# LayerNorm output turned by DMA in blocks 2 to 4 of an S4 + GeGLU layer, with six single PSUM banks and a new order

## The chip, the cores and the metric

The kernel runs on one core of a Trainium2 chip. The core has a matmul engine (TensorE, PE in the profile, with its weight loads as PEld), VectorE (DVE), ScalarE (ACT), GpSimd (POOL) and SyncE (SP), which issues most of the transfers; 16 DMA engines move the data. Each engine works through its own list of instructions in order. The metric is the time of one execution on the device, in microseconds (us), as the median of the runs.

## The reference

One layer of a state-space model with adaptive LayerNorm: length 2048, width 448, state 256, hidden width 1792.

```python
mod = (silu(c) @ w_mod).reshape(c.shape[0], 6, 1, -1)
sa, ca, ga, sb, cb, gb = (mod[:, 0], ..., mod[:, 5])
h = layernorm(x) * (1 + ca) + sa
# A: K[d, l] = Re sum_n C * exp(dt * A * l) * dt * B, then a causal convolution of h with K by FFT, + h * Dskip
x = x + ga * A(h)
h = layernorm(x) * (1 + cb) + sb
# B: gelu(h @ w_gate) * (h @ w_up) @ w_down
x = x + gb * B(h)
```

All inputs and the output are float32.

## The kernel before

**The front** makes the convolution filters K from tables (sine, cosine, exponent on ACT, products on DVE, sums on PE), transforms h and K, multiplies and transforms back. `k_fft` is the part of it that the change touches: for three frequencies at a time it multiplies a filter spectrum in PSUM (pk) with the input spectrum (ut), in `prod`, with one DVE multiply for each of two copies of the input.

**The back** is the gated network, in four blocks of 512 positions; the text calls them blocks 1 to 4, the code has `blk` 0 to 3. For each block, `conv_out` finishes the convolution on PE (co.mm, `yi` times `ai`), adds it to x and takes the LayerNorm (co.add, co.rt, co.rc, co.n) in four parts j of 128 positions. The normalised rows xn (positions on the partitions) must then be turned so that the width lies on the partitions, and split into two fp16 halves, high and low, for exact products: the tile `ht`, 128 x (8 groups of columns) x 4 parts x 128 positions. Block 1 turns float32 rows on PE and splits after (co.t, co.h, co.l). Blocks 2 to 4 split first, into `hl` (high half by ACT or DVE, co.h2; low half by DVE, co.l2), and turn the eight 128x128 fp16 squares on PE with the identity `idenh` into a PSUM tile pt (co.t2, `tr16`); one ACT or DVE copy brings pt to ht (co.c2).

`gate_up` then makes 14 tiles of 128 hidden units: gate and up products on PE in two PSUM banks (pq), GELU on ACT, product on DVE into fq, fp16 split into hh and hlo (`hg`). `down_first` (block 1) and `down` (the others) multiply with w_down; `down` saves matmuls by sums of quarters, in seven products dn0 to dn6 that share three banks. Gate and up weights are split once, kept in DRAM (w_d) and loaded again for each block (wr<-w_d).

**The order** is not the code's. Every step is given to a planner (`Plan`) with an estimated cost for the engines that could run it, what it depends on, and the tiles that it uses; a table `LEAD` shifts the priority of each kind of step, `LEAN` its choice between ACT and DVE. The planner walks through an imagined execution and writes each engine's list of instructions. PSUM has eight banks: in the back, 2 of pt, 2 pairs of pq, 2 of pd (conv-out and down).

The line numbers of the profile before are those of this code:

Of the kernel before, what the change touches and what calls it, by code (L numbers as in the profile page):

```python
# [39 lines left out]
    "anc": -11.71, "ang": -3.44, "bn": 2.2, "c.ai": 5.1, "c.ak": 11.34, "c.au": 12.5, "c.c": 9.28, "c.ea": -19.79,  # L40
    "c.id": -13.24, "c.ih": -0.48, "c.ld": 6.17, "c.rd": -9.5, "co.add": 158.93, "co.adde": -601.4,
    "co.addl": 221.1, "co.addx": 274.52, "co.c2": -159.69, "co.h": 1162.42, "co.h2": -38.47, "co.l": 75.87,
    "co.l2": -285.37, "co.mm": 1062.5, "co.mme": -3.27, "co.mml": 286.81, "co.mmx": 500.21, "co.n": -262.48,
    "co.nx": -202.79, "co.rc": 141.8, "co.rcx": 932.59, "co.rt": 19.25, "co.rtx": -646.04, "co.t": 495.31,
    "co.t2": -516.32, "cos": 5.17, "cos2": 15.48, "d.hi": 901.84, "d.ld": 145.61, "d.lo": 186.95, "d0": -1.9,
# [3 lines left out]
    "e.f": -83.54, "e.hi": 186.89, "e.ld": 60.75, "e.lo": -179.4, "ev.end": -14.36, "ev.fp": -2.28, "ev.geg": 7.98,  # L49
    "ev.ub": -1.24, "f.fc": -5.91, "f.fwd": 10.64, "f.inv": 3.75, "f.pr": -22.92, "f.st": -1.52, "f.ut": 3.93,  # L50
    "f.z": 6.62, "gs": 6.11, "gu": 492.6, "gu.g": -553.63, "gu.h0": 585.93, "gu.ha": -745.69, "gu.hs": -215.61,
    "gu.l0": -34.07, "gu.la": -409.31, "gu.ls": 228.5, "gu.m": 128.51, "gu.s": -35.53, "gu2": -791.75, "ka": 22.04,
    "kd": -6.07, "kev": 9.93, "kgen": 14.34, "kout": 18.8, "lt0": -6.27, "lt1": 1.35, "m.ev": -4.31, "m.ld": 12.22,
# [4 lines left out]
    "p.q31": 2.88, "p.q32": -17.5, "p.q33": -6.64, "pad": 14.21, "rcp": 3.06, "rstd": 1.67, "silu": 10.66,  # L58
    "sin": 8.04, "sin2": 21.53, "t.fc": 12.26, "t.fwd": -1.68, "t.inv": 4.48, "t.p0": -3.04, "t.p1": -11.75,
    "t.st": -18.59, "t.u": 6.08, "t.z": 9.25, "tx": 2.71, "tyc": 5.88, "tys": 1.61, "ua": -6.43, "ua.ev": -7.17,  # L60
    "ua.st": -3.05, "ub": 21.06, "ub.ev": 16.13, "ub.fc": -8.54, "ub.st": 6.94, "ub.u": 2.75, "w.hi": -6.17,
    "w.ld": 2.03, "w.lo": -8.97, "warm": 9.58, "wr.ld": -4.52, "wr.st": 12.94, "x.exp": 2.24, "x.ld": 10.88,
    "x.mm": -1.83, "x1.ld": 7.86, "y.exp": 6.27, "y.mm": -1.56, "yi.d00": -4.27, "yi.d01": 7.83, "yi.d10": -18.27,
    "yi.d11": -8.15, "yi.e": -7.12, "yi.l0": -7.58, "yi.l1": 7.22, "yi.ld": -12.53,
}
LEAN = {
    "co.c2": -0.272, "co.h": -0.408, "co.h2": -0.264, "f.z": -0.511, "kev": -0.043, "kout": -0.269, "mag": -0.072,
    "p.q0": -0.54, "p.q2": -0.299, "p.q30": -0.133, "p.q32": 0.295, "t.z": -0.367, "ua.ev": 0.406, "ub.ev": -0.643,
# [24 lines left out]
class Plan:  # L93


    TABLE, HOP, STICK, RATE = 1.3, 0.3, 5.57, 280.0
# [90 lines left out]
def constants():  # L187
# [45 lines left out]
    for i, e in enumerate(EORD):  # L233
# [35 lines left out]
        "k_ih": np.eye(128, dtype=np.float16),  # L269
# [4 lines left out]
def s4_geglu(ctx: ExitStack, tc: tile.TileContext, a: dict, out: bass.AP):  # L274
# [51 lines left out]
                 "ak0": 1, "ak1": 1, "tp": 4, "w": WST, "yi": 1, "x1": 2, "pd": 2, "pt": 2, "pq": 2,  # L326
                 "ht": 1, "xn": 3, "hl": 2, "ge": 2, "fq": 2, "hg": 1, "wr": WR})
# [545 lines left out]
    def ev_end():  # L873
# [6 lines left out]
        K2["ih"] = POOLS["yp"].tile([128, 128], HF, name="idenh", bufs=1)  # L880
# [7 lines left out]
    def k_fft(grp, bi):  # L888
# [28 lines left out]
        def prod():  # L917
            for t in range(2):
                V.tensor_mul(pp.tile[:, t, :ne], ut.tile[:, t, :ne], pk.tile[:, :ne])  # L919
# [19 lines left out]
        t4 = add("f.pr", {"DVE": 1.22 * f}, v, prod, [t3, t2], [], [pk, ut, pp])  # L939
# [214 lines left out]
    def conv_out(blk, t_x, t_y):  # L1154
# [55 lines left out]
        for j in range(4):  # L1210
            xn, pt, hl = Buf("xn"), Buf("pt"), Buf("hl")
# [6 lines left out]
            def tr(pt=pt, xn=xn):  # L1218
                pt.tile = POOLS["ps"].tile([128, 4, 128], FT, name="pt")
                for k in range(3):  # L1220
                    T.matmul(pt.tile[:, k], xn.tile[:, 128 * k:128 * k + 128], K2["id"], start=True, stop=True)
                for h in range(2):
                    T.matmul(pt.tile[64 * h:64 * h + 64, 3], xn.tile[:, 384:], K2["id"], start=True, stop=True)
# [17 lines left out]
            def tr16(pt=pt, hl=hl):  # L1241
                pt.tile = POOLS["ps"].tile([128, 8, 128], HF, name="pt")
                for k in range(8):
                    T.transpose(pt.tile[:, k], hl.tile[:, 128 * k:128 * k + 128], K2["ih"])
# [20 lines left out]
    def gate_up(blk, f, half=None):  # L1265
# [8 lines left out]
        pb, gb = Buf("pq"), Buf("ge")  # L1274
# [9 lines left out]
        def mm():  # L1284
            ht = hb.tile.rearrange("p k j t -> p k (j t)")
            pb.tile = [POOLS["ps"].tile([128, 512], FT, name=f"pq{k}") for k in range(2)]

            def pair():
                for k in range(2):
                    r = slice(64 * k, 64 * k + 64)  # L1290
                    T.matmul(pb.tile[k][:, ts], wr.tile[r, 3, k, c0:c0 + 128], ht[r, 7, ts],  # L1291
# [3 lines left out]
            for k in range(2):  # L1295
                for i, (m, lo, t) in enumerate(full):
                    T.matmul(pb.tile[k][:, ts], wr.tile[:, 4 * lo + t, k, c0:c0 + 128], ht[:, m, ts],  # L1297
# [4 lines left out]
        def gelu():  # L1302
            gb.tile = POOLS["wk"].tile([128, 512], FT, name="ge")
            A.activation(gb.tile[:, ts], pb.tile[0][:, ts], AF.Gelu_apprx_tanh, scale=1.0 / WS)  # L1304

        def mul():
# [3 lines left out]
            src = [x[:, ts].rearrange("p (h t) -> p h t", t=256) for x in (gb.tile, pb.tile[1])]  # L1310
# [14 lines left out]
        def lo(c):  # L1325
            V.tensor_sub(hg.tile[1][:, cb, c], fq.tile[:, c], hg.tile[0][:, cb, c])  # L1326
        t1 = add("gu" + n, {"PE": 4.4 * w + 0.29}, v, mm, cps + WT[blk, cb] + [GU.get((blk, "g"))], [pb], [hb, wr])
        t2 = add("gu.g", {"ACT": 0.18 + 0.42 * w}, v + 0.9, gelu, [t1], [gb], [pb], table=GELU)
        t3 = add("gu.m", {"DVE": 0.15 + 0.54 * w}, v + 0.9, mul, [t2] + GU.get((blk, cb), []), [fq] if new else [],
                 [gb, pb] + ([] if new else [fq]))  # L1330
# [22 lines left out]
    def down_first(j):  # L1353
# [4 lines left out]
        def mm():  # L1358
            (hh, hl), (dh, dl) = hg.tile, W["d"]
            pb.tile = POOLS["pd"].tile([128, D], FT, name="pd")  # L1360
            ts = slice(128 * (j % 2), 128 * (j % 2) + 128)
            for p in range(7):
# [6 lines left out]
        def res():  # L1369
# [3 lines left out]
        t1 = add("dn", {"PE": 7.95}, v, mm, [GU[0, "l", p] for p in range(7)] + [WT["d", i] for i in range(7)] +  # L1373
                 [GU.get((0, "d"))], [pb], [hg])
# [4 lines left out]
    def down(blk):  # L1379

        hg, xb, pb, ab = HG[blk], X1[blk], Buf("pq"), Buf("pd")
# [3 lines left out]
        def bank(k):  # L1385
            return (ab.tile if k == 2 else pb.tile[k])[:, :D].rearrange("p (m d) -> p m d", m=2)

        def mm(i, q, k, new, ps):
            (hh, hl), (dh, dl) = hg.tile, W["d"]
            if i == 0 and ps[0] == 0:  # L1390
                pb.tile = [POOLS["ps"].tile([128, 512], FT, name=f"pq{x}") for x in range(2)]
                ab.tile = POOLS["pd"].tile([128, D], FT, name="pd")
# [22 lines left out]
        def prod(i, q, k, new, deps, v_, al=(), use=(), ps=range(7)):  # L1415
            return add("dn%d" % i, {"PE": 0.565 * len(ps)}, v + v_, lambda: mm(i, q, k, new, list(ps)), deps + wd, al, list(use) + [hg])

        def kept(n, k, deps, v_):
            b = Buf("xn")
            return b, add("dn.k" + n, {"ACT": 0.55}, v + v_ + 0.02, lambda: keep_(k, b), deps, [b], [ab if k == 2 else pb])  # L1420

        def out_(n, src, h, c, deps, v_):
# [3 lines left out]
                    [xb, ab if src[-1] == 2 else pb] + ([] if one else [ob]))  # L1426
# [7 lines left out]
        p1 = prod(0, (0, 0), 0, True, la[:6] + [g], 0.0, [pb, ab], (), range(6))  # L1434
        p1 = prod(0, (0, 0), 0, False, la[6:] + [p1], 0.1, (), [pb], (6,))
# [129 lines left out]
```

## Time and profile before

| | us |
|---|---|
| median of three runs | 831.16 |
| their range | 828.82 to 837.64 |
| the profiled execution | 839.22 |
| its span, first to last instruction | 837.4 |
| PE busy | 752.7 (90%) |
| DVE busy | 606.6 (72%) |
| ACT busy | 463.4 (55%) |
| block 2's part of the back, 541.8 to 640.8 us | PE busy 99.0 of 99.0 |

A row of the profile names the line, the engine, the operation, and what it writes and reads by the program's names (pq<-ht,wr is a matmul of ht with wr into pq). SPq rows are SP's issues of transfers. "Idle before" is what an engine waited just ahead of the instruction, with who released it. A wait on an engine that is not the bottleneck costs nothing.

### The profile page before, as it was taken

To read this page: it belongs to the slowest core of one execution; us is meant where nothing else is said; L and a number is where in the kernel's file an instruction comes from. 1 tells how busy PE (TensorE), PEld (TensorE's weight loads), DVE (VectorE), ACT (ScalarE), POOL (GpSimd) and SP (SyncE) were. 2 spreads that over 40 slices of the span, in tenths; PEclk is the share of its full clock that TensorE was granted. 3 is DMA by queue.
4 is the path that set the end of the run, shared out by engine and by line. 5 is a ranking of instruction groups with operands and counts; after the bars stand their busy time and mean duration, and the time that the engine had idled before them with its cause. 6 is when DMAs were issued, how large, how long until landed. Compare 5 with 4: busy or idle time off the path is not lost.

```text
span 837.4 us, 19110 instructions
## 1 busy us (share of the span) xinstructions
PE 752.7 (90%) x8166; PEld 460.1 (55%) x8166; DVE 606.6 (72%) x1023; ACT 463.4 (55%) x608; POOL 8.4 (1%) x19
## 2 busy tenths in 40 slices
PE   0776888999899999988669999999999999999997
PEld 0334344444467776767637445544497445964477
DVE  4789998989979989896774767258883556745452
ACT  4598889998879999971134533034332332323320
POOL 1000000000000000000200000000000000000000
PEclk9889699999999999998969999999999999999999
DMA  9563367798748847799669761454415332022101
GB/s 273 125 176 122 88 185 200 222 275 265 225 141 233 249 108 218 245 306 285 163 227 266 276 220 56 115 183 132 154 57 120 135 127 78 27 77 88 44 12 35
DMA packets 93183, 136.78 MB, mean 163 GB/s; under 512 B 22576, under 2 KB 75600, under 8 KB 93098
## 3 DMA queue, kind: packets, MB, share of 16 engines
q1 hardware_dynamic: 89850, 132.77, 52.6%
q10 hardware_dynamic: 2608, 1.61, 0.7%
q8 instruction: 64, 1.05, 0.5%
q0 software_dynamic: 640, 1.18, 0.4%
q14 instruction: 21, 0.17, 0.1%
HBM read 100.42 MB, written 36.01 MB: 163 GB/s over the span
## 4 chain that ended last, share of the span: by engine, by line
PE 67%; ACT 16%; DVE 7%; DMA 5%; issue 3%; SPq 1%; ACTq 0%; DVEq 0%
PE pq L1297 30%; PE pq L1397 9%; PE pd L1366 4%; ACT fg L566 3%; PE pg L553 3%; PE pf L824 3%; PE kg L633 3%; PE pf L692 3%; ACT my L540 2%; ACT fg L558 2%; ACT fg L570 2%; PE pq L1291 2%; PE pf L1012 2%; PE pf L926 2%; PE pd L1397 1%
## 5 line engine op out<-in xcount | busy, mean ns | idle before, releaser
L1297 PE MATMUL pq<-ht,wr 128*128 128x512 f16 (+1 forms) x1200 | 251.2, 368 | 0.8 <-DVE ht L1231 0.8
L1297 PEld LDWEIGHTS <-wr 128*128 128x128 f16 x1200 | 115.5, 99 | 131.1 <-issue 13.5
L1311 DVE TENSOR_TENSOR fq<-ge,pq 128x512 f32<-128x512 f32 (+1 forms) x60 | 39.1, 651 | 92.7 <-PE pq L1297 64.5
L1304 ACT ACTIVATE ge<-pq 128x512 f32<-128x512 f32 (+1 forms) x60 | 34.1, 568 | 100.4 <-PE pq L1291 58.9
L1323 ACT ACTIVATE hh<-fq 128x1024 f16<-128x1024 f32 (+1 forms) x49 | 47.2, 963 | 64.4 <-DVE fq L1311 50.5
L1397 PE MATMUL pq<-d,hh 128*128 128x224 f16 x504 | 73.3, 259 | 0.0
L602 DVE TENSOR_TENSOR tx<-mx,fg 128x1024 f32<-128x1024 f32 x56 | 67.6, 1220 | 6.2 <-PE kg L633 5.3
L633 PE MATMUL kg<-ty,tx 128*32 128x64 f32 x3584 | 61.7, 220 | 10.6 <-DVE ty L610 5.6
L606 DVE TENSOR_TENSOR ty<-my,fg 128x1024 f32<-128x1024 f32 x56 | 68.2, 1219 | 2.5 <-ACT fg L570 1.7
L633 PEld LDWEIGHTS kg<-ty,tx 128*32 128x32 f32 x3584 | 52.8, 110 | 27.7 <-issue 14.0
L1397 PE MATMUL pq<-d,hlo 128*128 128x224 f16 x252 | 65.3, 259 | 0.0
L566 ACT ACTIVATE fg<-pg 128x1024 f32<-128x1024 f32 x56 | 56.5, 1020 | 2.6 <-PE pg L553 1.6
L540 ACT ACTIVATE my<-pg 128x1024 f32<-128x1024 f32 x56 | 55.5, 1045 | 3.3 <-PE pg L535 3.1
L1397 PEld LDWEIGHTS <-hh 128*128 128x128 f16 x588 | 56.5, 98 | 0.8 <-issue 0.3
L1326 DVE TENSOR_TENSOR hlo<-fq,hh 128x1024 f16<-128x1024 f32 (+1 forms) x49 | 54.0, 1103 | 3.2 <-ACT hh L1323 3.0
L926 PE MATMUL pf<-q,fc 128*128 128x160 f32 x264 | 43.3, 316 | 0.7 <-DVE q L919 0.7
L926 PEld LDWEIGHTS pf<-q,fc 128*128 128x128 f32 x264 | 38.1, 197 | 6.7 <-issue 2.0
L553 PEld LDWEIGHTS <-lt 64*128 64x128 bf16 x336 | 20.4, 95 | 38.8 <-issue 24.7
L553 PE MATMUL pg<-ea,lt 64*128 64x512 bf16 x168 | 34.4, 392 | 7.4 <-ACT fg L566 5.7
L692 PE MATMUL pf<-fg,c_sb 112*128 112x448 f32 x48 | 21.3, 597 | 19.7 <-DMA fg<-in_w_mod 19.7
L609 DVE SCALAR_TENSOR_TENSOR ty<-my,fg 128x512 f32<-128x512 f32 x56 | 38.3, 685 | 0.2 <-ACT fg L566 0.2
L610 DVE TENSOR_TENSOR ty<-my,fg 128x512 f32<-128x512 f32 x56 | 38.4, 685 | 0.0
(177 smaller groups left out, 1204.6 us busy)
## 6 DMA issues: line engine op xcount, KB each, us to landing
wr<-w_d SPq DMA_DIRECT2D x21, 896.0 KB, 5.7
fc<-in_k_fc SPq DMA_DIRECT2D x20, 576.0 KB, 4.7
u_d<-so SPq DMA_DIRECT2D x32, 224.0 KB, 3.0
w<-in_wgu SPq DMA_DIRECT2D x14, 512.0 KB, 5.5
ui<-u_d SPq DMA_DIRECT2D x10, 672.0 KB, 6.2
w_d<-wr SPq DMA_DIRECT2D x7, 896.0 KB, 7.3
fq<-in_wd SPq DMA_DIRECT2D x14, 448.0 KB, 3.7
us<-uo SPq DMA_DIRECT2D x22, 240.0 KB, 6.1
```

The source lines that it names most:

```text
L540: A.activation(yb.tile.rearrange("p a b c -> p (a b c)"), pb.tile, AF.Exp)
L553: T.matmul(pa[:, nh * 512:nh * 512 + 512], w, x, start=(k == 0), stop=(k == 2))
L566: A.activation(fb.tile[:, 0].rearrange("p x (n k) -> p n x k", n=2), pb.tile.rearrange("p (n x k) -> p n x k", n=2, x=2), AF.Sin, scale=TW ...
L602: V.tensor_mul(tx.tile, xb.tile[:, xm, None, :].to_broadcast([128, 2, 512]), fb.tile[:, :, 0])
L606: V.tensor_mul(ty.tile[:, 1], yb.tile, fy()[:, 1, :, None, :].to_broadcast([128, 16, 2, 32]))
L633: T.matmul(kg[32 * g:32 * g + 32, 2 * (s % 2) + q, :64], tx[:, r, nh, 4 * q + g], ty[:, r, nh, 4 * q + g], start=(r == 0 and nh == 0), sto ...
L692: T.matmul(pb.tile, c_sb[:, t:t + 1].to_broadcast([DT, 128]), wb.tile[:, t], start=(t == 0), stop=(t == 3))
L926: T.matmul(pz.tile[:, e % 32 - sl0], fc.tile[:, i, 1 + t], pp.tile[:, t, i], start=(t == 0 and e != 32), stop=(t == 1 and e != 0))
L1297: T.matmul(pb.tile[k][:, ts], wr.tile[:, 4 * lo + t, k, c0:c0 + 128], ht[:, m, ts], start=f % 2 == 0 and i == 0, stop=f % 2 == 1 and i == 9)
L1323: A.activation(hg.tile[0][:, cb, c], fq.tile[:, c], AF.Copy)
L1326: V.tensor_sub(hg.tile[1][:, cb, c], fq.tile[:, c], hg.tile[0][:, cb, c])
L1397: T.matmul(bank(k)[:, m], x[:, p, q[0], ts], w[:, p, q[1]], start=new and m == 0 and p == 0 and z == 0, skip_group_check=True, stop=i in ( ...
```

## The change

The transposes on PE and the copies behind them (co.t2, co.c2) are replaced in blocks 2 to 4 by eight transposing transfers for each part, from hl straight to ht, issued by SP. The identity `idenh` and its load go. The planner may hold two ht tiles, where it had one. The pairs of pq banks and the two pt tiles become one pool of six single banks. Block 1's down tiles are planned in two pieces (hidden groups 0 to 5, and 6). In `k_fft` the two multiplies become one of twice the length. LEAD, LEAN and one constant of the planner have new numbers, of which two lines stand here.

```diff
-    "co.l2": -285.37, "co.mm": 1062.5, "co.mme": -3.27, "co.mml": 286.81, "co.mmx": 500.21, "co.n": -262.48,
+    "co.l2": -275.5899, "co.mm": 1067.0718, "co.mme": 20.4646, "co.mml": 270.9186, "co.mmx": 512.094,
...
-                 "ak0": 1, "ak1": 1, "tp": 4, "w": WST, "yi": 1, "x1": 2, "pd": 2, "pt": 2, "pq": 2,
-                 "ht": 1, "xn": 3, "hl": 2, "ge": 2, "fq": 2, "hg": 1, "wr": WR})
+                 "ak0": 1, "ak1": 1, "tp": 4, "w": WST, "yi": 1, "x1": 2, "pd": 2, "pq": 6,
+                 "ht": 2, "xn": 3, "hl": 2, "ge": 2, "fq": 2, "hg": 1, "wr": WR})
...
-            for t in range(2):
-                V.tensor_mul(pp.tile[:, t, :ne], ut.tile[:, t, :ne], pk.tile[:, :ne])
+            V.tensor_mul(pp.tile[:, :, :ne].rearrange("p t e d -> p t (e d)") if ne == 3 else pp.tile[:, :, :ne],
+                         ut.tile[:, :, :ne].rearrange("p t e d -> p t (e d)") if ne == 3 else ut.tile[:, :, :ne],
+                         (pk.tile.rearrange("p e d -> p (e d)") if ne == 3 else pk.tile[:, :ne])[:, None].to_broadcast(
+                             [128, 2, 3 * n] if ne == 3 else [128, 2, ne, n]))
...
-        POOLS["ps"] = ctx.enter_context(tc.tile_pool(name="ps", bufs=2, space=PSUM))
+        POOLS["ps"] = ctx.enter_context(tc.tile_pool(name="ps", bufs=6, space=PSUM))
...
-            def tr16(pt=pt, hl=hl):
-                pt.tile = POOLS["ps"].tile([128, 8, 128], HF, name="pt")
-                for k in range(8):
-                    T.transpose(pt.tile[:, k], hl.tile[:, 128 * k:128 * k + 128], K2["ih"])
-
-            def out_(e, j=j, pt=pt):
+            def turn(j=j, hl=hl):
                 if j == 0:
                     hb.tile = POOLS["wk"].tile([128, 8, 4, 128], HF, name="ht")
-                cp(e, hb.tile[:, :, j], pt.tile)
+                for k in range(8):
+                    dma(hb.tile[:, k, j], hl.tile[:, 128 * k:128 * k + 128], transpose=True)
...
-                t4 = add("co.t2", {"PE": 0.55}, vj + 0.3, tr16, [t3, c_ih], [pt], [hl])
-                cps.append(add("co.c2", {"ACT": 1.05, "DVE": 0.75}, vj + 0.4, out_, [t4] + cps[:1], [hb] if j == 0 else [],
-                               [pt] + ([hb] if j else [])))
+                cps.append(add("co.t2", {"SP": 3.4}, vj + 0.3, turn, [t3] + cps[:1], [hb] if j == 0 else [],
+                               [hl] + ([hb] if j else []), kb=256))
...
-            pb.tile = [POOLS["ps"].tile([128, 512], FT, name=f"pq{k}") for k in range(2)]
+            for b in pb:
+                b.tile = POOLS["ps"].tile([128, 512], FT, name="pq")
...
-        t1 = add("dn", {"PE": 7.95}, v, mm, [GU[0, "l", p] for p in range(7)] + [WT["d", i] for i in range(7)] +
-                 [GU.get((0, "d"))], [pb], [hg])
+        t1 = add("dn", {"PE": 6.815}, v, lambda: mm(range(6)), [GU[0, "l", p] for p in range(6)] + [WT["d", i] for i in range(6)] +
+                 [GU.get((0, "d")), GU[0, "g"]], [pb], [hg])
+        t1 = add("dn", {"PE": 1.135}, v, lambda: mm((6,)), [GU[0, "l", 6], WT["d", 6], t1], (), [pb, hg])
```

How the lists of instructions change is shown at three places. The changed kernel's lines are 2 to 5 numbers higher (L1144 wr<-w_d is L1149 there, L1429 out<-x is L1432). The first is SP's list at the end of block 2's gate stage and through its down stage, ahead of block 3: before,

```order
L1471 DMA fq<-in_wd 128x4x224
L1144 DMA wr<-w_d 128x3584
L1429 DMA out<-x_5696 128x2x224 x3
L1060 DMA yi<-y_67 64x2x640 x2
L1060 DMA yi<-y_68 64x2x640 x2
L1060 DMA yi<-y_69 64x2x512 x2
L1429 DMA out<-x_5696 128x2x224
```

and now:

```order
L1473 DMA fq<-in_wd 128x4x224
L1149 DMA wr<-w_d 128x3584
L1250 DMA_TRANSPOSE ht<-hl 128x128 x8
L1432 DMA out<-x_5611 128x2x224
L1250 DMA_TRANSPOSE ht<-hl 128x128 x24
L1432 DMA out<-x_5611 128x2x224 x2
L1065 DMA yi<-y_67 64x2x640 x2
L1065 DMA yi<-y_68 64x2x640 x2
L1065 DMA yi<-y_69 64x2x512 x2
L1432 DMA out<-x_5611 128x2x224
```

The 32 transfers for block 3 stand between the last load of its first gate weights (wr) and the output stores of block 2; three stores and the convolution inputs of block 4 (yi) are behind them. For block 4 the place is the same. For block 2 they stand behind block 1's first output store:

```order
L1149 DMA wr<-w_d 128x3584
L1380 DMA out<-x_5174 128x448
L1250 DMA_TRANSPOSE ht<-hl 128x128 x24
L1380 DMA out<-x_5174 128x448
L1250 DMA_TRANSPOSE ht<-hl 128x128 x8
L1380 DMA out<-x_5174 128x448
```

Three parts of block 2 go ahead of block 1's second store, the fourth behind it. The second place is PE's list at the start of block 3's gate stage, with its waits (a DMAHW name is one of eight counters of landed transfers). Before:

```order
L1397 MATMUL pq_6996<-d_5864,hlo 128x224
L1297 LDWEIGHTS wr [waits DMAHW1_49]
L1297 MATMUL pq_7404<-ht,wr 128x512 [waits Activation_49]
L1297 LDWEIGHTS wr
L1297 MATMUL pq_7404<-ht,wr 128x512
```

Now:

```order
L1399 MATMUL pq<-d_5866,hlo 128x224
L1298 LDWEIGHTS wr [waits DMAHW6_49,DMAHW0_49]
L1298 MATMUL pq<-ht,wr 128x512 [waits DMAHW5_49]
L1298 LDWEIGHTS wr
L1298 MATMUL pq<-ht,wr 128x512 [waits DMAHW7_49]
L1298 LDWEIGHTS wr
L1298 MATMUL pq<-ht,wr 128x512 [waits DMAHW0_49]
L1298 LDWEIGHTS wr
L1298 MATMUL pq<-ht,wr 128x512 [waits DMAHW1_49]
```

Where the first gate matmul waited for the last ACT copy, each of the first seven now waits for one landed transfer; between the down products that stand ahead, the transposes are gone. The third place is DVE's list in the same down stage, the split of parts 1 to 3 of block 3, where L1243 and L1244 make the low half and L339 the high half:

```order
L1243 TENSOR_TENSOR hl<-xn,hl 128x448 [waits DMAHW4_49,DMAHW2_49,Activation_49]
L1244 COPY hl<-hl 128x64 [waits DVE_49]
L1220 SCALAR_TENSOR_TENSOR xn<-x_6515,mv_6849,rows 128x448
L1221 SCALAR_TENSOR_TENSOR xn<-xn,rs_6850,rows 128x448 [waits DVE_49]
L339 CAST hl<-xn 128x448 [waits DMAHW4_49,DMAHW5_49,DMAHW3_49,DMAHW6_49,DMAHW2_49,DMAHW7_49,DMAHW1_49,DMAHW0_49]
L339 CAST hl<-xn 128x64
L1243 TENSOR_TENSOR hl<-xn,hl 128x448 [waits DVE_49]
L1244 COPY hl<-hl 128x64 [waits DVE_49]
L339 CAST hl<-xn 128x448 [waits DMAHW4_49,DMAHW3_49,DMAHW5_49,DMAHW2_49,DMAHW6_49,DMAHW1_49,DMAHW7_49,DMAHW0_49,Activation_49]
L339 CAST hl<-xn 128x64
```

The high halves of parts 2 and 3 wait for all eight transfers of the part that had the hl tile before them, and DVE's next instructions, the output adds of block 2's down, stand behind these.

More of the change, by code (lines that the diff above doesn't have):

```diff
@@ L69 @@
+    "p.q0": -0.7061, "p.q2": -0.8412, "p.q30": 0.2141, "p.q32": -0.1013, "t.z": -0.3714, "ua.ev": 0.4433,
+    "ub.ev": -0.6201,
 }
@@ L938, in k_fft @@
         t3 = add("f.fwd", {"PE": 1.02 * f}, v, fwd, [t1, t2] + AKT[grp], [pk], [fc, AKB[grp]])
-        t4 = add("f.pr", {"DVE": 1.22 * f}, v, prod, [t3, t2], [], [pk, ut, pp])
+        t4 = add("f.pr", {"DVE": 1.09 * f}, v, prod, [t3, t2], [], [pk, ut, pp])
         t5 = add("f.inv", {"PE": 1.84 * f}, v, inv, [t4, t1], [pz], [fc, pp])
@@ L1290, in pair @@
                     r = slice(64 * k, 64 * k + 64)
-                    T.matmul(pb.tile[k][:, ts], wr.tile[r, 3, k, c0:c0 + 128], ht[r, 7, ts],
+                    T.matmul(pb[k].tile[:, ts], wr.tile[r, 3, k, c0:c0 + 128], ht[r, 7, ts],
                              start=f % 2 == 1, stop=f % 2 == 0)
@@ L1356, in down_first, with mm @@
         v = 114.0 + j
-        def mm():
+        def mm(ps):
             (hh, hl), (dh, dl) = hg.tile, W["d"]
-            pb.tile = POOLS["pd"].tile([128, D], FT, name="pd")
+            if ps[0] == 0:
+                pb.tile = POOLS["pd"].tile([128, D], FT, name="pd")
             ts = slice(128 * (j % 2), 128 * (j % 2) + 128)
-            for p in range(7):
+            for p in ps:
                 for z in range(2):
@@ L1385, in bank @@
         def bank(k):
-            return (ab.tile if k == 2 else pb.tile[k])[:, :D].rearrange("p (m d) -> p m d", m=2)
+            return pb[k].tile[:, :D].rearrange("p (m d) -> p m d", m=2)
         def mm(i, q, k, new, ps):
             (hh, hl), (dh, dl) = hg.tile, W["d"]
-            if i == 0 and ps[0] == 0:
-                pb.tile = [POOLS["ps"].tile([128, 512], FT, name=f"pq{x}") for x in range(2)]
-                ab.tile = POOLS["pd"].tile([128, D], FT, name="pd")
+            if new:
+                pb[k].tile = POOLS["pd"].tile([128, D], FT, name="pd") if k == 2 else POOLS["ps"].tile([128, 512], FT, name="pq")
             for m in range(2):
```

89 lines of the change are left out of this document (44 added, 45 removed), and 16 rows, old and new, of the table LEAD.

## The prediction

> **What bounds the kernel now.** I read first the page's share of each engine, then the same by stages. The windows below are the front (0 to 375 us: filters and transforms), the passage to the gated network (375 to 434), the gated network (434 to 833) and the end; columns are length, then busy us and count for PE, PEld, DVE, ACT and POOL, then the granted clock.
>
> ```profile
> PE 752.7 (90%) x8166; PEld 460.1 (55%) x8166; DVE 606.6 (72%) x1023; ACT 463.4 (55%) x608; POOL 8.4 (1%) x19
> ...
> 125.00:375.00 250.00, 232.16 (x4126) 151.06 (x4125) 226.24 (x338) 228.04 (x281) 0.00 (x0) 0.99 0.75 223
> 375.00:434.00 59.00, 40.56 (x433) 35.53 (x434) 41.01 (x75) 12.35 (x20) 5.62 (x10) 0.85 0.73 223
> 434.00:833.00 399.00, 398.05 (x2574) 232.08 (x2572) 234.44 (x411) 127.99 (x170) 0.00 (x0) 0.99 0.38 119
> ```
>
> From 434 us to the end TensorE is busy 398.05 of 399 us: that half is a chain of matmuls, and every instruction taken out of it is gained whole, as long as nothing makes TensorE wait. DVE (234 us) and ACT (128 us) have room there, and so has the DMA (share 0.38). Ahead of it, three engines are each busy over 90% of 125 to 375 us, so no one of them sets the time alone. What TensorE waited for after 434 us is one row:
>
> ```profile
> PE pq L1297 <- DVE ht L1231: 0.8, 1, 0.8
> ```
>
> **The change part by part.** First, what leaves TensorE. The chain in order of time shows block 3's conv-out and block 2's down stage; the timeline shows 16 transposes at once.
>
> ```profile
> 609.80 0.69 PE pd L1173 x4
> 610.49 0.22 PE pd L1178 x4
> 610.70 4.13 PE pq L1397 x42
> 614.84 4.03 PE pd L1397 x42
> 618.86 4.03 PE pq L1397 x42
> 622.88 0.45 PE pt L1244 x8
> 623.33 4.03 PE pq L1397 x42
> 627.36 0.89 PE pt L1244 x16
> 628.25 8.05 PE pq L1397 x84
> 636.30 0.45 PE pt L1244 x8
> 636.75 4.03 PE pq L1397 x42
> 640.77 4.32 PE pq L1297 x20
> ...
> 516.03 1.06 PE L1244 MATMUL pt<-idenh,hl 128*128 128x128 f16 x16
> 516.92 0.54 PE L1366 MATMUL pd<-d,hh 128*128 128x448 f16 x2
> ```
>
> Eight transposes (one part j of a block) hold TensorE for 0.45 us, and sixteen from 516.03 to 516.92, 0.89. There are 4 parts in each of 3 blocks: 12 x 0.445 = **5.3 us off the path**. Their evictions also go:
>
> ```profile
> L333 ACT ACTIVATE ht<-pt 128x1024 f16<-128x1024 f16 (+1 forms) x10 | 8.9, 893 | 30.2 <-PE pt L1244 25.9 <-PE pt L1223 2.2 <-issue 2.1
> L335 DVE COPY ht<-pt 128x1024 f16<-128x1024 f16 x5 | 3.4, 686 | 0.0
> ```
>
> Seven ACT copies of 1.02 us and five DVE copies of 0.69 leave engines that have room: worth nothing.
>
> Second, what comes in their place: 96 transfers of 128x128 on SP's queue, 32 for each block. They run during the down stage, since the LayerNorm needs all four conv-out parts and the last of those stands just before down (609.80). The trace has no transposing transfer, so its **pace p** (time from one to the next) must be bounded. In the order each transfer waits for the one eight before it, so p is the larger of its issue time and an eighth of its time to land. The nearest rows are SP's issue times (ns min/median/max) and the landing times of the same rows:
>
> ```profile
> L1144 SPq DMA_DIRECT2D wr<-w_d x21: 319/320/344, 485.9 to 776.9; - x21
> L908 SPq DMA_DIRECT2D q<-us x22: 314/430/802, 220.1 to 363.5; - x22
> L1081 SPq DMA_DIRECT2D yi<-y x8: 644/670/890, 401.7 to 419.4; - x8
> DMA to landing us min/median/max: 2.1/2.5/2.9
> DMA to landing us min/median/max: 4.3/5.0/7.0
> DMA to landing us min/median/max: 2.1/5.0/12.5
> ```
>
> (The landings are of the output stores L1429, of q<-us L908, and of everything that touches the x tiles, loads of 896 KB among them.) Issue medians run from 0.32 to 0.67 us, and the slowest landing of q<-us, 7.0 us, gives 7.0/8 = 0.875; the farthest row, 12.5/8, would be 1.56, but it is of a load 28 times as large. I take p = 0.5, the middle of the issue medians: 32 KB in rows of 256 bytes is a small transfer, like the q<-us rows (0.43). Ends kept for the range: 0.32 and 0.875.
>
> Is that hidden? Three more rows date the start; the first two are the fp16 halves of part 0 for block 3 (ACT then DVE), the third is SP waiting for block 1's stores.
>
> ```profile
> 618.57 0.72 ACT L333 ACTIVATE hl<-xn 128x448 f16<-128x448 f32 x2 [1.54 <-DVE xn L1216]
> 620.75 0.62 DVE L1238 TENSOR_TENSOR hl<-xn,hl 128x448 f16<-128x448 f32 x1
> 519.32 7.40 SPq L1377 DMA_DIRECT2D out<-x  x2
> ```
>
> Block 3: the high half is there at 618.57 + 0.72 = 619.3, so transfer 31 (the last that gate's first seven matmuls want, 0.22 us apart) is issued at 619.3 + 31p with one output store of 0.4 us between, and lands 2.5 us later: 622.2 + 31p. Down without its transposes ends at 640.77 - 4 x 0.445 = 639.0, and the seventh matmul is due at 640.3. So p may reach 18.1/31 = 0.58 us. I take block 4 to be the same. Block 2: part 0 stands behind block 1's first output store, issued at 519.32, and 0.9 us earlier without the 16 transposes; 31 transfers and a store land at 518.8 + 0.3 + 31p + 2.5 = 521.6 + 31p; block 1's down takes from 508.1 to
>
> ```profile
> 525.92 15.89 PE pd L1366 x84
> 541.81 4.32 PE pq L1297 x20
> ```
>
> 541.81, less 1.8, plus 1.3 to the seventh matmul: 541.3, so p up to 0.635. What TensorE loses is then **2 x (31p - 18.1) + (31p - 19.7)**, each term only where positive. At p = 0.5 it is nothing; at 0.32 also nothing; at 0.67, 2 x 2.7 + 1.1 = 6.4 us; at 0.875, 2 x 9.0 + 7.4 = 25.4 us. Two things stand behind these transfers. On SP, output stores and the next block's convolution inputs; those are wanted a whole gate stage later, as before. On DVE and ACT, the split of parts 2 and 3 now waits until parts 0 and 1 have landed (two hl buffers), and behind it on DVE stand the output adds of down; part 1 lands at 619.3 + 0.4 + 16 x 0.5 + 2.5 = 630.2, ahead of the next output add in the trace (its row is DVE L1407 at 632.38, below), so it costs nothing at my p.
>
> ```profile
> 632.38 0.62 DVE L1407 TENSOR_TENSOR xn<-xn,pq 128x448 f32<-128x448 f32 x1 [2.58 <-PE pq L1397]
> ```
>
> [...]
>
> Third, six PSUM banks taken singly, two ht tiles and the first down tile cut in two: each would shorten a TensorE wait, and after 434 us there is only the 0.8 us above. Nothing, and nothing lost: the eight banks (2 pt, 4 pq, 2 pd) stay eight. The loads of block 3's first weights stand before the transfers on SP, as they stood before the stores.
>
> Fourth, the product in the transform stage, one multiply of 960 for two of 480:
>
> ```profile
> L919 DVE TENSOR_TENSOR q<-q,pf 128x480 f32<-128x480 f32 x44 | 26.6, 649 | 4.3 <-PE pf L915 4.3
> L561 DVE TENSOR_SCALAR fg<-pg 128x1024 int32<-128x1024 int32 x3 | 3.7, 1220 | 0.8 <-PE pg L553 0.8
> ```
>
> From 480 elements at 0.649 to 1024 at 1.220 is 1.05 ns an element, so 960 take 1.15 us; 22 of them 25.4 instead of 26.6. Of 1.2 us on an engine that is one of three full ones I count half, 0.6.
>
> Fifth, the new order of the front. The load on ACT and DVE hardly changes (in the order eleven copies of the front go from ACT to DVE and seven back, and the table loads stay 42), so I take 0. Its bounds: in 125 to 375 us ACT idles 250 - 228.04 = 22 us and in 375 to 434 TensorE idles 18.4; a new order could win or lose a part of these, and I allow 10 us each way.
>
> **Sum.** The profiled execution took 839.22 us, 837.4 of span and 1.8 around it. 839.22 - 5.3 - 0.6 = 833.3. The median of the runs is 831.16, 8.06 lower; with the same distance I forecast **825 us**, 0.7% faster, inside the 1% that a measurement of this kernel can tell from no change (its three runs span 828.82 to 837.64).
>
> **The rivals.** *A: the transposing transfers are too slow for the down stage, and TensorE waits at the start of gate in blocks 2 to 4.* It decides from p = 0.665: there 93p - 55.9 equals the 5.9 us won. Over 1% slower begins at p = 0.75. At 0.875, the far end of the rows, the result is 825.2 + 25.4 = 851 us. For it: the margin is only 0.08 us of pace over my value in blocks 3 and 4, and 32 issues on one in-order queue stand where four stores stood. Against: every issue median is at or below 0.67. [...]
> *B: the new order of the front wins as well.* If it fills a quarter to a half of the idle 22 us of ACT, it brings 5 to 10 us: 815 to 820. For it: three engines near 91% leave gaps that are only a matter of order. Against: the sequence at the start and at the passage is nearly that of before.
> *C: the exchange cancels.* p between 0.58 and 0.75 loses up to 14 us against 5.9 won: 826 to 839, around 831. It is also what is seen if the transposes leave but TensorE waits as long as they lasted.
>
> **How the numbers follow.** My forecast (820 to 828) 0.38, B 0.22, C 0.11, A 0.29. Faster by over 1% (below 822.8) is B and a little of the forecast, 0.25; slower by over 1% (above 839.5) is A, 0.29, and the front lost, 0.02; within 1% the rest, 0.44. The range must take in most of A: to p = 1.06 it loses 2 x 14.8 + 13.2 = 43 us, 868, and I leave out its tail beyond (to 1.56, 89 us) at 0.10; below, B to 816. Beside it, the forecast with B and C alone spans 815 to 839.
>
> **What would show it.** In the profile after: no L1244-like PE rows, 96 transposing issues on SP, and their p between issues; TensorE in the down stage busy without a gap, and the first gate matmul of blocks 2 to 4 starting within 1 us of down's last. If instead it waits there for the DMA of ht, A is right and the wait times three is its price. If the gated network shortens by 5 us and the total does not, the front has lost it. A pace above 0.58, or a LayerNorm that comes later than 619.3 - 610.7 = 8.6 us after down's start, makes the forecast wrong.

## The result and the profile after

The changed kernel takes **907.72 us** (median of 4 runs, 901.42 to 912.82) against 831.09 of before: a ratio of 1.0904, 95% interval 1.081 to 1.0999. The forecast was 825, with a range of 816 to 868. Rival A has come, at a price beyond the end that I had left it. The profiled execution took 909.43 us with a span of 907.6.

First the page's share of each engine, then the same stages as before the change (columns as above: length; busy us and count for PE, PEld, DVE, ACT, POOL; granted clock, DMA share, GB/s).

```profile
PE 771.1 (85%) x8070; PEld 462.3 (51%) x8070; DVE 602.5 (66%) x995; ACT 457.5 (50%) x602; POOL 8.4 (1%) x19
...
125.00:375.00 250.00, 233.12 (x4012) 149.65 (x4006) 226.33 (x323) 226.98 (x275) 0.00 (x0) 0.97 0.75 217
375.00:434.00 59.00, 41.24 (x541) 36.52 (x540) 40.59 (x72) 12.25 (x22) 5.62 (x10) 0.83 0.77 239
434.00:833.00 399.00, 343.26 (x2006) 188.00 (x2006) 202.10 (x357) 107.19 (x146) 0.00 (x0) 0.91 0.39 122
833.00:907.00 74.00, 70.04 (x494) 45.84 (x490) 32.04 (x52) 17.10 (x23) 0.00 (x0) 0.99 0.11 38
```

Of 434 to 833 us TensorE is now busy 343.26, where it was busy 398.05, and 70 us of work are left after that; the front reads as before. What TensorE waits for from 434 us on (us in total, times, longest) was a single row of 0.8 us. Now it is:

```profile
PE pq L1298 <- DMA ht<-hl: 38.4, 21, 11.6
PE pq L1399 <- DVE xn L1409: 6.6, 1, 6.6
PE pq L1399 <- ACT xn L1415: 5.2, 2, 4.2
PE pq L1399 <- ACT hh L1324: 4.3, 1, 4.3
PE pq L1226 <- DVE xn L1221: 2.9, 1, 2.9
PE pq L1399 <- DVE hlo L1327: 0.8, 1, 0.8
```

The first row is gate (L1298) waiting for a transposed part, as rival A said. Those of L1399 are waits inside down, which the prediction had put at nothing; L1226 belongs to block 1's turning. The cause of the first stands in SP's rows for the transfers (count, issue time in ns min/median/max) and in SP's timeline at block 2:

```profile
L1250 SPq DMA_TRANSPOSE ht<-hl x96: 1101/1222/1933, 518.9 to 807.9; - x96
```
```profile
518.41 0.34 SPq L1380 DMA_DIRECT2D out<-x  x1
518.85 30.55 SPq L1250 DMA_TRANSPOSE ht<-hl  x24
549.44 0.58 SPq L1380 DMA_DIRECT2D out<-x  x1
550.13 10.52 SPq L1250 DMA_TRANSPOSE ht<-hl  x8
560.75 0.52 SPq L1380 DMA_DIRECT2D out<-x  x1
561.37 3.77 SPq L1065 DMA_DIRECT2D yi<-y  x6
```

One transfer holds SP for 1.222 us, and the pace is 30.55 / 24 = 1.27 us (1.31 with the store, 41.8 us for 32), not 0.5. The start, 518.85 us, is the predicted 518.8, in part by luck: block 1's down had begun 0.9 us later than before (509.01 against 508.1 us). The chain of waits shows how the row of issues ends in gate:

```profile
556.88 1.22 SPq L1250
558.15 2.38 DMA ht<-hl
560.58 4.92 PE pq L1298 x14
```

Gate's first matmul of block 2 starts at 552.48 us, where it started at 541.8 before, and then one after the other waits for its transfer; the seventh, the last that waits, is the 560.58 of the chain. The 2.38 us from the last issue to the landing are like those of an ordinary transfer (2.5 in the prediction), which points to the issuing as what is slow, and not to the moving of the bytes; e3 below tests it.

### The profile page after: what moved, and what is told of

Same layout as the page of the kernel before. It is cut to its first block, busy times and chain, and to the rows that moved or that the text cites. A ratio compares the mean times of both kernels' runs of the same rounds, so it can differ in the third digit from the quotient of the medians.

```text
span 907.6 us, 19069 instructions
## 1 busy us (share of the span) xinstructions
PE 771.1 (85%) x8070; PEld 462.3 (51%) x8070; DVE 602.5 (66%) x995; ACT 457.5 (50%) x602; POOL 8.4 (1%) x19
## 4 chain that ended last, share of the span: by engine, by line
PE 38%; SPq 10%; DVE 5%; DMA 4%; issue 1%; ACT 0%; DVEq 0%; ACTq 0%
PE pq L1298 25%; SPq L1250 9%; PE pq L1399 4%; PE pf L1017 2%; PE pq L1292 2%; DMA ht<-hl 2%; PE pf L1001 1%; PE pd L1178 1%; PE pd L1368 1%; PE pd L1399 1%; DMA fq<-in_wd 1%; DMA wr<-w_d 1%; PE pq L1226 1%; DVE hlo L1327 1%; DMA yi<-zo 0%
## 5 line engine op out<-in xcount | busy, mean ns | idle before, releaser
L1298 PE MATMUL pq<-ht,wr 128*128 128x512 f16 (+1 forms) x1200 | 260.1, 373 | 38.4 <-DMA ht<-hl 38.4
L1298 PEld LDWEIGHTS <-wr 128*128 128x128 f16 x1200 | 115.9, 99 | 177.9 <-issue 54.3
L1399 PE MATMUL pq<-d,hh 128*128 128x224 f16 x504 | 78.1, 269 | 16.1 <-DVE xn L1409 6.6
L637 PE MATMUL kg<-ty,tx 128*32 128x64 f32 x3584 | 64.0, 224 | 11.6 <-DVE ty L614 5.7
L637 PEld LDWEIGHTS kg<-ty,tx 128*32 128x32 f32 x3584 | 55.0, 112 | 28.4 <-issue 13.8
L1399 PEld LDWEIGHTS <-hh 128*128 128x128 f16 x588 | 59.1, 102 | 19.3 <-issue 12.6
L1399 PE MATMUL pq<-d,hlo 128*128 128x224 f16 x252 | 67.6, 268 | 0.8 <-DVE hlo L1327 0.8
L931 PE MATMUL pf<-q,fc 128*128 128x160 f32 x264 | 41.1, 306 | 0.8 <-DVE q L921 0.7
L696 PE MATMUL pf<-fg,c_sb 112*128 112x448 f32 x48 | 21.6, 606 | 19.4 <-ACT q L440 19.4
```

The costliest lines, as they stand in the source:

```text
L637: T.matmul(kg[32 * g:32 * g + 32, 2 * (s % 2) + q, :64], tx[:, r, nh, 4 * q + g], ty[:, r, nh, 4 * q + g], start=(r == 0 and nh == 0), sto ...
L931: T.matmul(pz.tile[:, e % 32 - sl0], fc.tile[:, i, 1 + t], pp.tile[:, t, i], start=(t == 0 and e != 32), stop=(t == 1 and e != 0))
L1298: T.matmul(pb[k].tile[:, ts], wr.tile[:, 4 * lo + t, k, c0:c0 + 128], ht[:, m, ts], start=f % 2 == 0 and i == 0, stop=f % 2 == 1 and i == 9)
L1399: T.matmul(bank(k)[:, m], x[:, p, q[0], ts], w[:, p, q[1]], start=new and m == 0 and p == 0 and z == 0, skip_group_check=True, stop=i in ( ...
```

## The experiments

Theory T: the 96 transfers cost the time, by their number and their pace on SP. Rival R: the other edits carry a part. Inside T stand two readings, a price for each *instruction* (I) or for each *square* of 128x128 (S), and beside it that the queues behind the transfers are the larger loss (Q). Differences below are those of the ratios to before, which was run beside each set (medians 832.78 to 836.24), times 833 us.

**e1: TensorE's transposes back, everything else as changed.**

```diff
-                cps.append(add("co.t2", {"SP": 3.4}, ..., turn, ...))
+                t4 = add("co.p2", {"PE": 0.55}, ..., tr16, [t3, c_ih], [pt], [hl])
+                cps.append(add("co.c2", {"ACT": 1.05, "DVE": 0.75}, ..., out_, ...))
```

> The changed kernel, with TensorE's transposes and the copies of ht back in blocks 2 to 4; the new order of the front, the six single banks, the first down tile in two parts and the merged product stay. Theory T (the 96 transposing transfers alone cost the time): about 831 of before, less 0.6 for the product, with nothing for the rest: 826 to 834 us. Rival R (the other edits carry a part: the new order, or banks that are taken later): it stays above 840; with half of the 77 us in them, about 870.

839.22 us, ratio 1.0081 (1.0053 to 1.011). The transfers carry 8.2% (68.5 us) of the 9.0%, but R is not empty: the other edits, which I had put at a gain of 0.6 us, are 0.8% slower than before.

**e2: the old kernel with the 96 transfers alone.**

```diff
-                for k in range(8):
-                    T.transpose(pt.tile[:, k], hl.tile[:, 128 * k:128 * k + 128], K2["ih"])
-...
-                cp(e, hb.tile[:, :, j], pt.tile)
+                for k in range(8):
+                    dma(hb.tile[:, k, j], hl.tile[:, 128 * k:128 * k + 128], transpose=True)
```

> The kernel before, with nothing changed but its transposes of blocks 2 to 4, which become 96 transfers on SP's queue. Theory T: the whole loss is here, 831 + 77 = 900 to 912 us. Rival R: 831 + 40 or less, below 875.

896.5 us, 1.0745 (1.0695 to 1.0794), 62 us above before: T, though 3.5 us short of the lower end of what it said; the other edits have a part of their own (e1).

**e3: the changed kernel, one transfer of 128x1024 for each part in place of eight squares.** All other instructions keep their places.

```diff
-                for k in range(8):
-                    dma(hb.tile[:, k, j], hl.tile[:, 128 * k:128 * k + 128], transpose=True)
+                dma(hb.tile[:, :, j], hl.tile, transpose=True)
```

> The changed kernel with one transposing transfer of 128x1024 for each part in place of eight of 128x128: 12 instead of 96, same bytes, every other instruction in its place. Theory I (the 1.22 us is a price for each instruction on SP): the four of a block take some 5 to 10 us, gate finds its ht, and the time is 822 to 835 us. Theory S (the price is for each 128x128 square, wherever it is paid): one issue or landing takes about 8 x 1.28 = 10 us, TensorE waits as before, and the time stays at 895 to 910 us.

838.98 us, 1.0062 (1.0024 to 1.01): 70 us are gone with the bytes unchanged. The issue row of this kernel beside that of the changed one decides between I and S:

```profile
L1249 SPq DMA_TRANSPOSE ht<-hl x12: 1231/1260/1573, 511.0 to 729.4; - x12
```

1.26 us for 256 KB, 1.22 for 32 KB: **the price is for the instruction**. The time is 4 us above theory I's interval, at the level of e1; what TensorE still waits for in its gated network is in block 2's down:

```profile
PE pq L1398 <- ACT hh L1323: 4.2, 1, 4.2
PE pq L1398 <- DVE hlo L1326: 0.8, 1, 0.8
```

**e4: the changed kernel with transfers in block 4 alone, TensorE's transposes in blocks 2 and 3.**

```diff
-                if True:
+                if blk != 3:
                     t4 = add("co.p2", {"PE": 0.55}, ..., tr16, [t3, c_ih], [pt], [hl])
```

> The changed kernel with transposing transfers in block 4 alone, TensorE's transposes in blocks 2 and 3. Nothing of the down weights is loaded any more there. Theory T with the pace alone: 2 x ... of one block only, 31 x 1.28 - 18.1 = 21.6 us less 1.8 for the transposes that leave: about 20 us above the kernel with TensorE's transposes everywhere, some 846 to 852. Rival Q (most of the loss is in the queues behind the transfers, late down weights above all): less than 12 us above it, under 842.

862.62 us, 1.034 (1.0285 to 1.0394): 21.6 us above e1 by the ratios, 23.4 by the medians, and three such blocks, 65 to 70, are the 68.5 between e1 and the changed kernel. Each block pays for itself, with no down weights late behind it: Q falls as the main loss.

**e5: TensorE's transposes and the other edits, with the order numbers of before.**

```diff
-    "co.l2": -275.5899, "co.mm": 1067.0718, "co.mme": 20.4646, ...
+    "co.l2": -285.37, "co.mm": 1062.5, "co.mme": -3.27, ...
```

> The kernel with TensorE's transposes and all the other edits, but with the order tables of before: up to the first gate its engines run the old sequence, only with the merged product. Theory F (the new order of the front costs some 7 us: gate begins at 434.56 us in the kernel with TensorE's transposes, profiled at its median, against 428.07 in the old front with the transposing transfers, also at its median): 831 to 833 us, a ratio of 0.996 to 1.001. Rival G (the six single banks or the cut first tile cost it): it stays at 838 to 840, a ratio of about 1.008.

875.15 us, 1.0527 (1.0479 to 1.0575): neither theory. The old numbers with the six banks set TensorE's transposes ahead of their input,

```profile
PE pq L1252 <- ACT hl L334: 24.9, 5, 10.8
```

so the run says nothing on the front; it was replaced by e9.

**e6: the changed kernel with the late down weights loaded from POOL's queue.**

```diff
-                dma(wb.tile[:, :4, :D2], a["wd"][i])
+                (P.dma_start if late else dma)(wb.tile[:, :4, :D2], a["wd"][i])
```

> The changed kernel, 96 transfers as they are, but the seven loads of the late down weights (L1473) are issued on POOL's queue, which has nothing to do there, instead of SP's behind the transfers. Theory Q (what the wait formula does not give, 5 to 10 us, is in these late loads: block 2's down waits 4.3 us for hh, and conv-out of block 3 comes late): 896 to 902 us. Rival K (it is in the lower clock after each wait, 269 against 259 ns a matmul): no change, 905 to 910.

911.29 us, 1.0933 (1.0892 to 1.0974), no gain, and the wait for hh in block 2's down is longer, not gone:

```profile
PE pq L1399 <- ACT hh L1324: 6.3, 1, 6.3
```

Theory Q falls: SP's queue is not what makes these loads late. On POOL's queue the last of them still waits for its tile, fq, which DVE's hlo frees:

```profile
626.34 0.75 POOL L1473 DMA_DIRECT2D fq<-in_wd  x1 [12.72 <-DVE hlo L1327]
```

**e7: the kernel before with only its transposes changed, to twelve wide transfers** (e2 with e3's edit).

> The kernel before with nothing changed but its transposes of blocks 2 to 4, as twelve transfers of 128x1024. Theory I (a price for each instruction; four a block are hidden): the 5.3 us of TensorE's transposes are won, 825 to 828 us, a ratio of 0.993. Rival Q (with the order of SP that the transfers bring, late down weights come later and block 2's down waits some 4 to 5 us, as it does in the changed kernel with wide transfers): nothing is left, 831 to 834, a ratio of 1.000.

**826.06 us, 0.9927 (0.99 to 0.9954): faster than both kernels**, and TensorE waits for nothing after 434 us. The issue and landing rows:

```profile
L1244 SPq DMA_TRANSPOSE ht<-hl x12: 1231/1258/2076, 504.1 to 719.3; - x12
DMA to landing us min/median/max: 3.1/3.1/3.1
```

e2 and e7 have every instruction in the same place but for the number of transfers: 96 against 12 cost 8.2%, 68 us. The groups by line show where: gate's own rows (count, busy us, mean ns, idle us ahead of them) of e2 and then of e7.

```profile
L1292 PE MATMUL pq<-ht,wr 128*128 128x512 f16 (+1 forms) x1200 | 264.1, 377 | 41.7 <-DMA ht<-hl 40.8 <-DVE ht L1231 0.8
```
```profile
L1291 PE MATMUL pq<-ht,wr 128*128 128x512 f16 (+1 forms) x1200 | 249.4, 366 | 0.0
```

Besides the wait itself, e2's gate matmuls are booked 14.7 us longer. The mean granted clock was 0.82, 0.80 and 0.70 in the three windows of e2's trace that hold these waits (540 to 580, 640 to 700 and 760 to 800 us), and 1.00 in every window of e7's from 434 to 800 us. Whether the longer matmuls are a lower clock after a wait is what e10 asks.

**e8: e7 with the late down weights on POOL's queue** (e6's edit).

> The same (old order, twelve wide transfers) with the late down weights on POOL's queue. Theory Q: the wait in block 2's down goes, 824 to 828 us, a ratio of 0.991 to 0.995. Rival P (issued on POOL they land later or collide with the transfers): 831 or more.

829.0 us, 0.9953 (0.9923 to 0.9984). It overlaps e7; no gain to be seen, and in e7 there was no wait to take away.

**e9: e7 with the changed kernel's order numbers ahead of the gated network, and its merged product.** The edit takes the new entries of the two order tables for all names but those of the gated network, the planner's new constant, and the product's lines.

> The kernel with the old code and twelve wide transfers (826.06 us), but with the changed kernel's order numbers for everything ahead of the gated network, and its merged product; the numbers of the gated network stay the old ones. Theory F (the new order of the front costs 6 to 7 us): 831 to 834 us, a ratio of 0.998 to 1.002. Rival G (it is the six banks and the order of the gated network that cost it): 825 to 828, a ratio of 0.993.

831.01 us, 0.9982 (0.9952 to 1.0011), 0.55% (4.6 us) above e7, just inside what theory F said and on its side. The two intervals touch, so the size is rough.

**e10: e2 with sixty more matmuls ahead of gate's first in blocks 2 to 4.**

```diff
+            if blk and f == 0:
+                for _ in range(60):
+                    T.matmul(pb.tile[0][:, :], wr.tile[:, 0, 0, :128], ..., start=True, stop=True)
```

> The kernel before with the 96 transfers alone (896.5 us), and in blocks 2 to 4 sixty more matmuls of 128x512 ahead of gate's first, on the weights that are there already; they write a bank that gate's first matmul starts anew. They take about 60 x 0.216 = 13 us each time, inside a wait of some 20. Theory K (a TensorE that has waited gets a lower clock, and the slower matmuls after it are the part of the loss that the wait formula lacks): the mean gate matmul goes from 377 ns back towards 366, and the time falls to 880 to 890 us. Rival N (the longer matmuls only contain the wait for the transfers): 893 to 900 us.

894.1 us, 1.0728 (1.0683 to 1.0773): 2.4 us under e2, with intervals that overlap. The row shows the matmuls shorter (371 ns, 7 us in all) and the wait filled,

```profile
L1298 PE MATMUL pq<-ht,wr 128*128 128x512 f16 (+1 forms) x1200 | 256.8, 371 | 10.2 <-DMA ht<-hl 7.9 <-DVE fq L1312 2.2
```

but the end hardly moves: the time is rival N's. Its mechanism is not shown by that, because the sixty matmuls took the low clock away in one block only. These are the fourteen gate matmuls behind the last awaited transfer, first of e2's block 3, then of e10's blocks 2 and 3:

```profile
673.51 4.94 PE L1292 MATMUL pq<-ht,wr 128*128 128x512 f16 x14 [0.66 <-DMA ht<-hl]
```
```profile
546.38 3.18 PE L1298 MATMUL pq<-ht,wr 128*128 128x512 f16 x14 [0.89 <-DMA ht<-hl]
668.75 4.87 PE L1298 MATMUL pq<-ht,wr 128*128 128x512 f16 x14 [0.87 <-DMA ht<-hl]
```

At the 0.216 us of the rows before the change fourteen would take 3.0 us. In e2 they take 5.5, 4.9 and 5.1 us in the three blocks; in block 3 the granted clock is 0.50 from 666 to 677 us, that is between gate's first seven matmuls and beyond them, and 1.00 from 678.5 us on. So about 6.5 us of e2's loss are matmuls at the lower clock behind the wait. In e10 the clock stays at 1.00 in block 2, but in blocks 3 and 4 it is down to 0.50 again (670 to 672 us, 790 to 794 us): gate's first matmuls still wait for single transfers behind the sixty. What was gained in block 2 went into a wait of gate for fq, the 2.2 us of the row above. How much of the 6.5 us a full clock would bring is therefore not shown.

**e11: e2 with four transfers of 128x256 a part, 48 in all.**

```diff
-                for k in range(8):
-                    dma(hb.tile[:, k, j], hl.tile[:, 128 * k:128 * k + 128], transpose=True)
+                for k in range(0, 8, 2):
+                    dma(hb.tile[:, k:k + 2, j], hl.tile[:, 128 * k:128 * k + 256], transpose=True)
```

> The kernel before with its transposes as four transfers of 128x256 for each part: 48 in all, 16 in a block. Theory I by the prediction's own formula, with 1.26 us an instruction: the 15 that gate's first seven matmuls want take 18.9 us against 18.1 of room in blocks 3 and 4 and 19.7 in block 2, a loss of 1.6 us, so 826 to 830. Rival S (a price by the square or the byte): half of the way to 896, 845 or more.

842.01 us, 1.0083 (1.0045 to 1.012), 13 us above e7 where the prediction's formula gave 1.6. Theory I holds for the issue (first row, 1.196 us), so S is out again; it is the formula's room that was too wide. Block 3's SP rows and the chain there show by how much:

```profile
L1245 SPq DMA_TRANSPOSE ht<-hl x48: 1182/1196/2304, 507.5 to 738.2; - x48
```
```profile
613.73 0.40 SPq L1424 DMA_DIRECT2D out<-x  x1
614.18 15.88 SPq L1245 DMA_TRANSPOSE ht<-hl  x12
630.51 0.39 SPq L1424 DMA_DIRECT2D out<-x  x1
631.01 5.55 SPq L1245 DMA_TRANSPOSE ht<-hl  x4
```
```profile
633.59 3.20 DMA ht<-hl
...
636.84 5.09 PE pq L1292 x16
```

Sixteen transfers with the store between them take 22.4 us (614.18 to 636.56), not the 18.9 of fifteen at 1.26, and they start behind an output store. Down had ended at 631.87; four of gate's matmuls go ahead between the waits, and the sixteen from 636.84 on take 5.09 us, 0.32 each instead of 0.216, and the mean granted clock from 610 to 645 us is 0.95, where e7 has 1.00 from 600 to 645 us. From the start of one down stage to the start of the next, e11 is 0.0, 5.8 and 7.8 us longer than e7, 13.6 in all.

**e12: e2 with three hl buffers.**

```diff
-                hl.tile = POOLS["wk"].tile([128, 1024], HF, name="hl")
+                hl.tile = POOLS["wk"].tile([128, 1024], HF, name="hl", bufs=3)
```

> The kernel before with the 96 transfers alone (896.5 us) and three hl buffers in place of two, so that the split of part 2 waits for no transfer. Theory H (splits that stand on DVE and ACT ahead of down's own evictions add to the loss; down waits 8.7 us for xn there): 885 to 890 us. Rival T (the transfers' pace sets the end of the stage whatever down does, the wait only moves to gate's start): 893 to 899 us.

896.39 us, 1.0758 (1.0715 to 1.08), the same as e2. Down's waits for xn (8.7 us in e2) are down to 0.7, and the wait moves to gate:

```profile
PE pq L1292 <- DMA ht<-hl: 52.4, 21, 16.0
...
PE pq L1392 <- DVE xn L1402: 0.7, 1, 0.7
```

Theory T: the waits inside down are no second loss. The end of the row of transfers sets the start of gate, however the wait before it is shared out.

**e13 and e14: the two mixed cases** of what is left between e3 and e9 (same front, wide transfers; they differ in the six banks with the cut first tile and the second ht tile, and in the order numbers of the gated network). e13 has the new numbers and the old banks, e14 the old numbers and the new banks.

> Wide transfers, the new order numbers throughout, but the old banks (two for the transposes, a pair for gate and up) and an uncut first down tile. Theory O (the new numbers of the gated network cost the 8 us, by a wait of block 2's down for hh): 837 to 841 us, a ratio of 1.006 to 1.010. Rival B (the banks and the cut tile cost them): 829 to 833, about 0.998.

> Wide transfers, the new order numbers up to the gated network and the old ones in it, with the six single banks and the cut first tile. Theory O: 829 to 833 us, a ratio of about 0.998. Rival B: 837 to 841, a ratio of 1.006 to 1.010. If both this and the other mixed kernel lie at 838, each of the two needs the other as it was.

851.57 us, 1.0204 (1.0165 to 1.0244), and 868.51 us, 1.0409 (1.0368 to 1.045): each mixture is slower than both pure cases, by waits of its own, e13's in the first row, e14's in the other two.

```profile
PE pq L1450 <- DVE fq L1464: 13.6, 1, 13.6
```
```profile
PE pq L1449 <- DVE fq L1463: 16.4, 1, 16.4
PE pq L1449 <- DMA ht<-hl: 15.4, 1, 15.4
```

Numbers and banks belong together, so this remainder can't be put on one of them.

## Why the prediction was wrong

Step by step the loss adds up, by the ratios: transposes off TensorE by wide transfers, e7, -0.73% (6.1 us won); the new front and the merged product, e9 against e7, +0.55% (4.6 lost); banks, cut tile, second ht tile and new order of the gated network, e3 against e9, +0.80% (6.7 lost); 96 transfers instead of 12, the changed kernel against e3, +8.42% (70 lost). That is the 9.04% measured, 75 us.

- *"I take p = 0.5, the middle of the issue medians."* **This step failed.** The measured issue is 1.222 us and the pace 1.27 to 1.31. The rows that I read, at 0.32 to 0.67 us, were of another kind of instruction, DMA_DIRECT2D; they bound nothing of DMA_TRANSPOSE, and my reason (32 KB is small) was about bytes, where e3 shows a price without bytes (1.26 us for 256 KB). My far end, 0.875, was as wrong for the same reason: it was a landing time divided by eight, and the landing, 2.3 us, is not what limits. The range's top, 868, stood for a pace of 1.06, still below the measured one; the 1.56 of the farthest row was left out as a tail.
- *The formula 2 x (31p - 18.1) + (31p - 19.7).* The mechanism and nearly the size were right. With 1.27 it gives 62 us, with 1.31 66, and e2 against e7 measures 68. Block by block it fits less well, and that the sums lie so close is in part luck: from the start of one down stage to the start of the next, e2 is 16.7, 26.1 and 25.5 us longer than e7, where the formula with 1.31 has 20.9, 22.5 and 22.5. In blocks 3 and 4 the start was put too early: I had the first transfer leave when its high half is ready, but the first output store of down stands ahead of it on SP and waits for an add on DVE. In e2, the high half's row and SP's:

```profile
627.64 0.72 ACT L333 ACTIVATE hl<-xn 128x448 f16<-128x448 f32 x2 [1.54 <-DVE xn L1216]
```
```profile
629.94 0.40 SPq L1424 DMA_DIRECT2D out<-x  x1
630.39 32.49 SPq L1245 DMA_TRANSPOSE ht<-hl  x24
```

  630.39 against 628.36 is 2.0 us, and block 4 has the same (753.63 against 751.61). The changed kernel loses this in its block 4: other than the text ahead of the prediction says, the place there is not that of block 3, a store goes first (766.59 us) and the transfers follow from 767.08 us. In block 2 of e2 the first eight transfers stand ahead of block 1's first store and leave 4.7 us after down's start (507.05 us), not 10.7, so less is lost there. And the formula lacks the lower clock behind the wait, some 2 us in each block of e2 (6.5 us in the three, by the rows under e10). For 48 transfers it stays too low for the same reasons (e11): late start, pauses between the parts, lower clock; their sum isn't worked out to the last microsecond.
- *"Two things stand behind these transfers ... so it costs nothing at my p."* At the true pace the splits did stand ahead of down's adds (6.6 and 5.2 us of waits), but e12 shows that it adds nothing to the total. The late down weights behind the transfers on SP add nothing that another queue would take away (e6).
- *"Third, six PSUM banks ...: nothing, and nothing lost."* **Wrong by 6.7 us**, together with the new order of the gated network, which I had not costed at all: I weighed the eight banks and saw that they stay eight, and of the new order looked only at the front. What shows is the wait for hh in block 2's down (4.2 us in e3, 4.3 after, none in e9). From the start of that stage to the start of block 3's, e3 takes 103.5 us and e9 96.3; the other two such stretches are equal. The trace of e3 shows why hh is late: the last of the late loads of down weights goes out at 602.52 us, 0.9 us after down's start, because it waits for the tile fq that DVE's hlo frees; in e9 it goes out 8.3 us ahead of down (598.11). DVE then waits for it, and the products that hh is made of stand behind this row on DVE:

```profile
606.20 0.39 DVE L1476 TENSOR_TENSOR fq<-fq 128x224 f32<-128x224 f32 x1 [3.11 <-DMA fq<-in_wd]
```

  Whether the banks or the order numbers make hlo so late stays open: the mixed cases don't separate them.
- *"Fifth, the new order of the front: 0, 10 us each way."* Measured +4.6 with the merged product, inside its bounds. Rival B, a gain of 5 to 10, fell. Only the medians carry this: gate starts at 438.4 us in the changed kernel's trace and at 430.2 in e3's, with the same instructions up to there.
- *"5.3 us off the path."* Right: e7 measures 6.1 (3.8 to 8.3). The forecast of 825 us is near what the exchange alone gives where the transfers are issued twelve times, 826.06; with the other edits it is 838.98 (e3).

## What to carry to other kernels

An operation that the trace doesn't contain isn't bounded by the rows of its neighbours (1.222 us here, where theirs were 0.32 to 0.67): where its price decides, the range must reach far beyond them. Count instructions on an issuing queue as one counts matmuls, and ask of a row of small transfers first whether one instruction can carry them all; here that alone turned 7.5% slower (e2) into 0.7% faster (e7). When a stage's end is set by a row of issues, waits that appear inside the stage can be the same loss seen earlier, as they were here; giving the row more buffers (e12) shows it at once. An experiment that is to take a low clock away should be read at the matmuls in question, and not by its total or its mean clock (e10). And a table of order numbers holds for the buffers it was made with: with others it cost 2 to 5% here.

## What the runs showed of the hardware

In these runs a transposing transfer from SBUF to SBUF took 1.20 to 1.26 us of SP's time, in the median, for 32, 64 or 256 KB (e2, e11, e3 and e7), some two to four times the 0.32 to 0.67 us of the ordinary rows, and its data landed 2.3 us (32 and 64 KB: e2, e11) or 3.1 us (256 KB: e7) later. In e2's block 3 the granted clock was 0.50 from 666 to 677 us, while gate's first seven matmuls waited for one transfer each and for 3.5 us from the seventh (673.51 us) on: the fourteen matmuls from there took 4.94 us, 5.5 and 5.1 in blocks 2 and 4, and 3.2 in e10's block 2, where sixty matmuls stood ahead of them and the clock was 1.00. The changed kernel's trace shows the same in block 2: the clock was 1.00 up to 542 us, 0.50 from 544 to 564 and 1.00 from 566 on; gate's first six matmuls took 0.58 or 0.59 us each there, and the fourteen from 560.58 us on took 4.92. Over the whole run the sixty raised the mean clock, their own time included, from 0.928 (e2) to 0.955 (e10), but lowered the total by no more than the runs can tell (894.1 against 896.5 us).
